# Channel mixing of the first batch element in plain block products, and Strassen weight sums made after it: an attention and mixer kernel on one Trainium2 core

## The chip, the cores and the metric

The kernel runs on one core of a Trainium2 chip. The metric is the device time of one execution in microseconds (us); less is better. One execution was also recorded by the hardware profiler, and all views of the profile come from it. The engines are named as there: PE is TensorE (PEld its weight loads), DVE is VectorE, ACT is ScalarE, POOL is GpSimd, and SP is the engine whose queue issues most of the transfers (DMAs).

## What is computed

Eight batch elements, each with 12 heads, 448 positions and a head size of 64, go through attention with normalized queries and keys. Its output, put together as 448 x 768 per element, goes through a mixer: first over the positions, then over the channels. The reference, cut:

```
def rmsnorm(x, g):
    rms = np.sqrt(np.mean(x * x, axis=-1, keepdims=True) + 1e-06)
    return x / rms * g
scores = scale * np.matmul(rmsnorm(q, g_q), rmsnorm(k, g_k).transpose(0, 1, 3, 2))
attn = np.exp(scores - np.max(scores, axis=-1, keepdims=True))
attn = attn / (np.sum(attn, axis=-1, keepdims=True) + 1e-09)
x = np.matmul(attn, v)                        # then (B, S, H*D)
h = np.maximum(x.transpose(0, 2, 1) @ w_tok1, 0.0) @ w_tok2
u = x + h.transpose(0, 2, 1)
out = u + np.maximum(u @ w_ch1, 0.0) @ w_ch2
```

All is float32, but the four weights come as float64; the kernel turns them into float32 itself, out of the bits of two 32-bit words. `w_ch1` is 768 x 1536, `w_ch2` 1536 x 768.

## The kernel before

**Start** (`Start.__init__`, L828) clears tiles, loads the queries and keys of the first two pairs of heads, and makes the norms of pair 0: `squares` (L900) squares on ACT and sums on DVE, `rsqrt` (L942) takes ten small DVE instructions. For pair 0 the queries' half is done first, then the keys'. A comparison of g_q and g_k picks one of two arms of the program (L986); with this data it is the one where `shifted` is False.

**Attention** goes by pairs of heads, six pairs to a batch element, 48 in all; two pairs take four steps (`att_step`, L461). A step has scores on PE, exponentials on ACT (`exp`, L291), and products with the values on PE (`av`, L397) for scores of the step before. Ahead of a pair's first step its queries are scaled (`scale`, L262, on POOL), and queries and keys are transposed on PE and copied by ACT (`trans_qk`, L274; in `before` that is an item of its own after the step, L532 to L534). Keys are not scaled; their norm goes into the exponential. From the second element on, the row sums are gathered by POOL and DVE (`chunk_sums`, L359).

**Mixing** of an element: transposes (`trans_x`, L553), `tok1` (L560), `tok2` (L571), which adds onto the element's tile `uT` in DVE (L579), then `ch1` (L635) and `ch2` (L689). The last two are Strassen products in Winograd's form: the weights and the moving matrix are cut into quarters, and seven products of half-size matrices, with sums of quarters before and after, take the place of eight. The moving sums are made by DVE and POOL (`moving_sums`, L587; in `ch1` L652 to L686), those after the products by L652 and L713. `ch2` comes as a double group (two of three column blocks) and a single one. A `ch1` item has two blocks of three matmuls of 224 columns, with 128 x 128 weights.

**Weights.** The two channel matrices come in 36 chunks, four that hold the token weights come before (`weight_chunks`, L118). A chunk is loaded by SP (`weight_load`, L145) into one of five `raw` tiles, goes through three instructions on DVE (`convert_first`, L189 to L192), two on ACT (`convert_second`, L200, L202), one on DVE (`convert_bits`, L209) and one on POOL (`convert_last`, L224), which leaves four quarters in a `stage` tile. `combine` (L160) then has POOL make the weights' sums of quarters, L163, L164 and L166, so that the tile has the seven stationary matrices; `store` (L168) writes them to a DRAM scratch (`ws1`, `ws2`, `ws3`). From there SP loads them again as `unit` tiles of 384 KB, five of them, for every one of the eight elements (`unit`, L608), in the order of `PRODUCTS` (L585). A unit is not loaded ahead before its group of chunks is stored.

**Order.** Each engine works through its instructions in the order in which they are written; there is no reordering. The order comes from `merge` (L29), which interleaves lists of items so that each list advances in proportion to the costs that stand beside its items. First come element 0's attention and 14 items of weights (L802); then, for each element, its mixing merged with the next element's attention (L805 to L820). In element 0 the rest of the weights is merged into the mixing too, so that the chunks of `w_ch1` and `w_ch2` are ready in time for their first use. SP's queue is written in the same way: a transfer that has to wait holds all behind it.

Of the kernel before, what the change touches and what calls it, by code (L numbers as in the profile page):

```python
# [22 lines left out]


NQ = 7
# [21 lines left out]
def whole(ctx, tc, shifted, pre, q, k, v, g_q, g_k, moe_w_tok1, moe_w_tok2, moe_w_ch1, moe_w_ch2, out):  # L47
# [28 lines left out]
    UNITS = 5  # L76
# [67 lines left out]

    def weight_load(i):  # L145
        rows, srcs, dst, split = chunks[i]
        n = columns(i) // len(srcs)
        wide = srcs[0].dtype == I64
        t = raw_pool.tile([P, WCOLS, 2] if wide else [P, WCOLS], U32 if wide else F32, name="raw")
        for k, src in enumerate(srcs):  # L150
            to = t[0:rows, k * n:(k + 1) * n]
            if wide:
                src = src.bitcast(U32)
                to = to.rearrange("p (i n) w -> p i (n w)", i=2) if dst is None else to.rearrange("p n w -> p (n w)")
            elif dst is None:
                to = to.rearrange("p (i n) -> p i n", i=2)
            nc.sync.dma_start(out=to, in_=src)
        st["raw", i] = t

    def combine(j):  # L160

        q = st["stage", j]
        nc.gpsimd.tensor_tensor(out=q[:, 6], in0=q[:, 1], in1=q[:, 0], op=ALU.subtract)  # L163
        nc.gpsimd.tensor_tensor(  # L164
            out=q[:, 4:6], in0=q[:, 1:7:5], in1=q[:, 3:4].to_broadcast([P, 2, P]), op=ALU.add)
        nc.gpsimd.tensor_tensor(out=q[:, 1], in0=q[:, 2], in1=q[:, 5], op=ALU.subtract)  # L166

    def store(j):  # L168


        w, group, m, t = stages[j]
        q = st.pop(("stage", j))
        if group < 3:
            to = ws1[group, :, :, t, m % 2, :]
        elif group == 3:
            to = ws3[:, :, t, :]
        else:
            to = ws2[t // 3, :, :, t % 3, m, :]
        nc.sync.dma_start(out=to.rearrange("q p n -> p q n"), in_=q[:])
        st["stored"] = j if j + 1 < len(stages) else j + 1  # L180

# [30 lines left out]
    def convert_last(i):  # L212
        rows, srcs, dst, split = chunks[i]
        n = columns(i)
        if dst is None:
            q = st["stage", i - len(first)] = stage_pool.tile([P, NQ, P], F32, name="stage")
            dst = q[:, 0:4, :].rearrange("p q n -> p (q n)")
        fold = (lambda a: a.rearrange("p (r c) -> p r c", c=split)) if split else (lambda a: a)
        t = st.pop(("raw", i))
        if srcs[0].dtype != I64:  # L220
            nc.gpsimd.tensor_copy(out=dst, in_=fold(t[0:rows, 0:n]))
        else:
            lo, hi = (fold(t[0:rows, 0:n, w].bitcast(F32)) for w in range(2))
            nc.gpsimd.tensor_tensor(out=dst, in0=lo, in1=hi, op=ALU.mult)  # L224
        if i >= len(first):
            combine(i - len(first))

# [34 lines left out]
    def scale(p):  # L262

        n = 2 * NS
        qk, rs = st["qk", p], st["rs", p]
        parts = [(R, 0, n, rs[0:R, 0:n].unsqueeze(2))]
        if shifted:
            parts.append((P, n, n - 2, rs[:, n:2 * n - 2].unsqueeze(2)))
            parts.append((P, 2 * n - 2, 2, rs[:, 2 * n - 2:2 * n - 1].unsqueeze(2)))
        for rows, o, m, r in parts:  # L270
            x = qk[0:rows, o * D:(o + m) * D].rearrange("p (r d) -> p r d", d=D)
            nc.gpsimd.tensor_tensor(out=x, in0=x, in1=r.to_broadcast([rows, m, D]), op=ALU.mult)  # L272

    def trans_qk(p, i):  # L274
        qk = st["qk", p]
        if i == 0:
            st["qkT", p] = qkT_pool.tile([P, S + NS * P], F32, name="qkT")
        ps = s_tile("t_ps")
        n = P if i else R
        for c in range(NS):  # L280
            o = (i * NS + c) * P
            nc.tensor.transpose(ps[:, c * n:(c + 1) * n], qk[0:n, o:o + P], ident[0:n, 0:n])  # L282
        to = st["qkT", p][:, S:S + NS * P] if i else st["qkT", p][:, 0:S]
        nc.scalar.mul(to, ps[:, 0:NS * n], g_t[:, i:i + 1])  # L284
        if i == 1:
            st.pop(("qk", p))
# [43 lines left out]
    def score_shifted(p):  # L330
# [4 lines left out]
        for c in range(NS):  # L335
            for a in range(2):
# [11 lines left out]
                pt = m_tile()  # L348
# [112 lines left out]
    def att_step(g):  # L461
# [48 lines left out]
        def tiled():  # L510
            if shifted:
                if live:
                    both_shifted()
                return
            if live:
                scores()
            products()

        items.append((3.75 if s in (0, 3) else 2.25, tiled))
# [12 lines left out]
        q = p + (s + 1) // 2  # L532
        if live and s % 2 == 1 and q < NP:
            items += [(0.4, lambda i=i: trans_qk(q, i)) for i in range(2)]  # L534
# [50 lines left out]
    PRODUCTS = ((0, "B11"), (2, "B21"), (5, "T2"), (6, "T3"), (4, "T1"), (1, "B22"), (3, "T4"))  # L585
# [14 lines left out]
    def unit_list(b):  # L600

        flat = lambda a: a.rearrange("p a b n -> p (a b n)")
        l = [(mp, flat(ws1[mp, q])) for mp in range(KF // 2) for q, _ in PRODUCTS]
# [4 lines left out]
    def unit(u):  # L608

        while st["loaded"] < min(u + UNITS, len(units)):  # L610
            i = st["loaded"]
            group, src = units[i]
            if st.get("stored", 0) < stage_end[group] and i > u:
                break
# [3 lines left out]
        return st.pop(("unit", u))  # L618

    def next_unit():  # L620
        st["at"] += 1
        return unit(st["at"] - 1)
# [8 lines left out]
    def put_off_done():  # L631
        while late_work:
            late_work.pop(0)()

# [118 lines left out]
    def middle_items(b):  # L753

        items = []
        for t in range(KC):
            items += [(us(NJ, S), lambda cc=cc: tok2(b, cc)) for cc in (t, KC + t)]
            items.append((0.0, lambda t=t: moving_sums(b, t)))
# [3 lines left out]
    def last_items(b):  # L762


        single = [(us(6, HS), lambda i=i: ch2(b, 1, i, 0)) for i in range(7)]
        l = turns(b, [0, 1, KC, KC + 1])
# [9 lines left out]
    st["loaded"] = st["at"] = 0  # L776
    r, late_work = {}, []
# [5 lines left out]

    load_v(0)
    weight_load(0)
    weight_load(1)
    scale(0)

    nc.vector.tensor_scalar(g_t[:, 0:1], g_t[:, 0:1], float(D) ** 0.5, None, ALU.mult)
    trans_qk(0, 0)  # L790
    trans_qk(0, 1)
# [4 lines left out]
    pre.squares(1, st)  # L796
    pre.roots(1, 1, st)
    swap(1)
    scale(1)
    per = NPAIR * 2  # L800
    att_items = lambda lo, hi: [it for g in range(lo, hi) for it in att_step(g)]
    for _, fn in merge(att_items(0, AHEAD * per + 1), weight_items(0, BEFORE)):  # L802
        fn()
    left = []
    for b in range(B):  # L805
        early, double = middle_items(b)
        if b == 0:
            begin = [it for h in range(2) for it in x_items(0, h) + tok1_items(0, h)]
            early = merge(begin + early, weight_items(BEFORE, then)) + merge(
                double, weight_items(then, len(chunks) + 3))  # L810
        else:

            for _, fn in merge(tok1_items(b, 0), left):
                fn()
            early = tok1_items(b, 1) + early + double
# [9 lines left out]
class Start:  # L825


    def __init__(self, ctx, tc, q, k, g_q, g_k, w2):  # L828
# [20 lines left out]
        for qk in [self.st["qk", p] for p in range(2)] + self.qk_t:  # L849
            nc.vector.memset(qk[96:P, 0:n // 2], 0.0)  # L850
            o = n - 2 * D
            nc.vector.memset(qk[D:P, o:o + D], 0.0)
            nc.vector.memset(qk[0:D, o + D:o + 2 * D], 0.0)
        self.load_qk(0, self.st, other=nc.scalar)
        self.load_qk(1, self.st)
# [15 lines left out]
        with tc.tile_pool(name="st_0", bufs=1) as self.st_pool:  # L871
            self.nt_pool = self.st_pool
            self.squares(0, self.st, halves=((0, 1), (1, 2)))
            self.st.pop(("ms", 0))

# [4 lines left out]
    def load_qk(self, p, st, other=None):  # L880
# [15 lines left out]
        for a in range(2):  # L896
            o = 4 * NS * D - 2 * D + a * D
            (other or self.nc.sync).dma_start(out=qk[a * D:(a + 1) * D, o:o + D], in_=self.k[b, hs][a][nk:])

    def squares(self, p, st, halves=((0, 2),)):  # L900
# [9 lines left out]
        for lo, hi in halves:  # L910
# [12 lines left out]
            if len(halves) > 1:  # L923
# [97 lines left out]
```

## Time and profile before

| | |
|---|---|
| median of 3 runs | 1482.06 us (1481.83 to 1483.47) |
| the profiled execution | 1482.08 us |
| its span, first to last instruction | 1480.3 us |
| PE busy, matmuls | 1394.3 us, 94% |
| DVE busy | 718.4 us, 49% |
| ACT busy | 470.7 us, 32% |
| POOL busy | 475.4 us, 32% |
| mean granted clock of PE | 0.975 |
| DMA | 214.77 MB, 145 GB/s mean |

How to read it: a busy share is a mean over the whole span, and the stages here differ. The views that follow give the span in 40 equal slices, each digit the busy share in tenths; a table by stretches of time, with the busy time of each engine, the number of its instructions, the clock that PE was granted (1 is full speed), the share of time that the 16 DMA engines were busy and what they moved; the waits of an engine, in total, how often, and the longest; and the chain of work that ended last, each line with its start, its length and what it was. A float32 matmul is two records on PE, so two MATMUL rows are one product. PE's busy time counts from issue to a modelled end and is longer where the clock is low.

### The profile page before, as it was taken

What the parts mean: (1) busy time and instruction counts of PE and PEld (TensorE: products, weight loads), DVE (VectorE), ACT (ScalarE), POOL (GpSimd) and SP (SyncE); (2) the same over time, 40 slices, a digit from 0 to 9 for tenths busy, and PEclk for the clock granted to TensorE, in tenths of its full rate; (3) what the DMA queues carried; (4) which work ended last, traced back from release to release, by engine and by line L of the source; (5) the groups of instructions that cost most, each with busy time, mean ns of one, the idle gap of its engine ahead of it and who ended that gap; (6) DMA issues with size and microseconds to landing.
All of it is one profiled execution on the core that took longest, in us unless ns stands there. A gap on an engine that the chain in (4) does not pass through costs nothing.

```text
span 1480.3 us, 19461 instructions
## 1 busy us (share of the span) xinstructions
PE 1394.3 (94%) x7048; PEld 1040.6 (70%) x7048; DVE 718.4 (49%) x1303; ACT 470.7 (32%) x802; POOL 475.4 (32%) x460
## 2 busy tenths in 40 slices
PE   5868767799999999999999999999999999999998
PEld 2324446586777867786777857777677947778998
DVE  7888897833454255433544345432544334331321
ACT  5654343322332234323342233322333223312111
POOL 2455686731233124321333123320332212310321
PEclk9988888899999999999999999999999999999999
DMA  6676677762455524553354625454354624444454
GB/s 151 168 213 183 192 238 216 212 196 84 122 149 144 159 76 138 147 151 112 106 155 127 181 56 153 132 152 130 103 148 124 179 62 128 122 124 134 128 172 135
DMA packets 235212, 214.77 MB, mean 145 GB/s; under 512 B 107140, under 2 KB 191620, under 8 KB 235108
## 3 DMA queue, kind: packets, MB, share of 16 engines
q1 hardware_dynamic: 211746, 202.20, 47.5%
q10 hardware_dynamic: 23234, 11.24, 2.7%
q8 instruction: 58, 0.95, 0.3%
q14 instruction: 46, 0.38, 0.1%
q0 software_dynamic: 128, 0.00, 0.0%
HBM read 185.86 MB, written 27.53 MB: 144 GB/s over the span
## 4 chain that ended last, share of the span: by engine, by line
PE 80%; POOL 1%; DMA 1%; DVE 1%; issue 1%; ACT 0%; SPq 0%; ACTq 0%; POOLq 0%
PE m_ps L704 26%; PE m_ps L647 23%; PE s_ps L302 7%; PE o_ps L403 6%; PE m_ps L566 5%; PE m_ps L574 4%; PE t_ps L545 3%; PE d_ps L382 2%; PE t_ps L282 2%; PE s_ps L316 1%; PE o_ps L415 1%; DMA unit<-ws 0%; POOL stage L224 0%; DMA ws<-stage 0%; POOL stage L164 0%
## 5 line engine op out<-in xcount | busy, mean ns | idle before, releaser
L704 PE MATMUL m_ps<-hb,unit 128*128 128x224 f32 x2016 | 402.7, 355 | 8.8 <-DMA unit<-ws 8.8
L704 PEld LDWEIGHTS m_ps<-hb,unit 128*128 128x128 f32 x2016 | 376.0, 191 | 28.7 <-issue 17.1
L292 ACT ACTIVATE e<-s_ps,rs 128x448 f32<-128x448 f32 x336 | 187.4, 633 | 214.2 <-PE s_ps L302 142.3
L647 PE MATMUL m_ps<-tu,unit 128*128 128x224 f32 x1152 | 238.9, 360 | 0.0
L647 PEld LDWEIGHTS m_ps<-tu,unit 128*128 128x128 f32 x1152 | 218.5, 194 | 15.7 <-PE o_ps L403 4.9
L647 PE MATMUL m_ps<-uT,unit 128*128 128x224 f32 x864 | 178.3, 359 | 9.3 <-DVE hb L652 6.1
L647 PEld LDWEIGHTS m_ps<-uT,unit 128*128 128x128 f32 x864 | 162.7, 192 | 28.8 <-issue 17.1
L302 PE MATMUL s_ps<-qkT 64*128 64x448 f32 x576 | 139.6, 588 | 5.9 <-ACT qkT L284 5.2
L272 POOL TENSOR_TENSOR qk<-qk,rs 112x512 f32<-112x512 f32 x46 | 51.1, 1132 | 265.5 <-DVE rs L951 189.2
L713 POOL TENSOR_TENSOR uT<-uT,r 128x448 f32<-128x448 f32 (+1 forms) x64 | 57.0, 901 | 245.6 <-DVE r L713 160.1
L403 PE MATMUL o_ps<-e,v 128*64 128x448 f32 x576 | 132.1, 562 | 0.0
L363 POOL TENSOR_TENSOR es<-e 128x896 f32<-128x896 f32 x42 | 88.3, 2102 | 63.3 <-ACT sq L913 47.6
L713 DVE TENSOR_TENSOR uT<-uT,m_ps 128x448 f32<-128x448 f32 (+1 forms) x80 | 38.9, 502 | 130.0 <-PE m_ps L704 127.8
L652 DVE TENSOR_TENSOR r<-m_ps,r 128x448 f32<-128x448 f32 x72 | 44.8, 622 | 117.6 <-POOL r L652 67.1
L566 PE MATMUL m_ps<-x,w_sb 112*128 112x384 f32 x256 | 92.4, 508 | 9.5 <-DVE x L551 9.5
L444 DVE STREAM_TRANSPOSE dt<-d_ps 128x448 f32<-128x448 f32 x42 | 27.3, 650 | 152.3 <-PE d_ps L382 152.3
L284 ACT ACTIVATE qkT<-t_ps,g_t 128x448 f32<-128x448 f32 x96 | 60.6, 657 | 127.3 <-PE t_ps L282 127.2
L369 DVE TENSOR_TENSOR es<-es,e 128x896 f32<-128x896 f32 x42 | 48.0, 1143 | 106.6 <-ACT e L292 75.8
L302 PEld LDWEIGHTS s_ps<-qkT 64*128 64x128 f32 x576 | 49.7, 191 | 68.3 <-issue 54.6
L403 PEld LDWEIGHTS o_ps<-e,v 128*64 128x64 f32 x576 | 33.0, 137 | 87.8 <-issue 85.0
L653 ACT ACTIVATE hb<-hb 128x448 f32<-128x448 f32 x72 | 41.7, 579 | 156.2 <-DVE hb L652 132.6
L574 PE MATMUL m_ps<-w_sb,h 128*128 128x448 f32 x192 | 80.0, 562 | 6.6 <-DVE uT L579 6.6
(85 smaller groups left out, 1478.2 us busy)
## 6 DMA issues: line engine op xcount, KB each, us to landing
unit<-ws SPq DMA_DIRECT2D x336, 384.0 KB, 3.2
raw<-in_moe_w_ch_dram SPq DMA_DIRECT2D x72, 256.0 KB, 3.3
ws<-stage SPq DMA_DIRECT2D x36, 448.0 KB, 3.3
out_dram<-y ACTq DMA_DIRECT2D x48, 224.0 KB, 3.3
qk<-in_q_dram SPq DMA_DIRECT2D x92, 112.0 KB, 3.2
v<-in_v_dram SPq DMA_DIRECT2D x48, 192.0 KB, 2.8
qk<-in_k_dram SPq DMA_DIRECT2D x92, 96.0 KB, 3.2
raw<-in_moe_w_tok_dram SPq DMA_DIRECT2D x4, 448.0 KB, 5.1
```

The costliest lines, as they stand in the source:

```text
L272: nc.gpsimd.tensor_tensor(out=x, in0=x, in1=r.to_broadcast([rows, m, D]), op=ALU.mult)
L284: nc.scalar.mul(to, ps[:, 0:NS * n], g_t[:, i:i + 1])
L292: nc.scalar.activation(out=out, in_=ps[:, 0:S], func=AF.Exp, scale=st["rs", p][:, r:r + 1])
L302: nc.tensor.matmul(out=pss[a][:, 0:S], lhsT=qkT[a * D:(a + 1) * D, o:o + P], rhs=qkT[a * D:(a + 1) * D, 0:S], start=True, stop=True)
L363: nc.gpsimd.tensor_tensor(out=es[:], in0=st["e", p, 0][:], in1=st["e", p, 1][:], op=ALU.add)
L369: nc.vector.tensor_tensor(out=es[:], in0=es[:], in1=st["e", p, 2][:], op=ALU.add)
L403: nc.tensor.matmul(out=o[a * D:(a + 1) * D, 0:S], lhsT=vt[:, c:c + D], rhs=e[:, a, :], start=start, stop=stop)
L566: nc.tensor.matmul(out=ps[:, 0:HC], lhsT=w1_sb[0:R, c, jc * P:(jc + 1) * P], rhs=st["x", h][0:R, c, :], start=(c == 0), stop=(c == NS - 1))
L574: nc.tensor.matmul(out=ps[:, 0:S], lhsT=st["h1", jc][:, cc * P:(cc + 1) * P], rhs=w2_sb[:, jc].rearrange("p c r -> p (c r)"), start=(jc == ...
L647: nc.tensor.matmul(out=ps[:, j * HS:(j + 1) * HS], lhsT=w[:, t, j, :], rhs=m, start=(t == 0), stop=(t == KC - 1))
L704: nc.tensor.matmul(out=ps[:, j * HS:(j + 1) * HS], lhsT=st["w"](j, t), rhs=hb[:, HB[what], t, :], start=(t == 0), stop=(t == KF - 1))
L713: add = lambda e, o, x, y: e.tensor_tensor(out=o, in0=x, in1=y, op=ALU.add)
```

## The change

Four things are done.

1. **Element 0's channel mixing** takes the eight plain products: `ch1_first` and `ch2_first` multiply the stored quarters with all 448 columns of `uT` and add up in PSUM. No moving sums and no sums after are made for element 0, but one addition per column block of the result. Element 0 uses 24 units in place of 42.
2. **The weights' sums** leave the conversion: `combine` is gone, a chunk is stored as four quarters. `sum_items` makes the sums afterwards, 40 items for 36 stages: an item reads a stage's four quarters back from DRAM into one of the five `raw` tiles, makes a subtraction on DVE, two additions in one on POOL and a subtraction on DVE for the three stages before, and writes the four sums of the stage before those. Eight items are merged into the double part of element 0, the rest into `tok2` and `ch1` of element 1. The scratch has eight slots a stage. There are six `unit` tiles, and `load_units` is called in the sum items too.
3. **The start**: the tiles' clearing is cut down and partly moved to POOL, an ACT instruction at the very start brings the table load forward, the keys of pair 0 are transposed first, the queries' norms come ahead of the keys', the queries of pair 0 are scaled on DVE. The norms and scaling of pair 1 come after the first attention step.
4. **The transposes of the next pair** stand between scores and products of a step, in place of after it, in the attention of element 0 (`inside`).

The diff, cut to its core:

```
-NQ = 7
+NQ = 8
-    UNITS = 5
+    UNITS = 6
...
-    def combine(j):
-
-        q = st["stage", j]
-        nc.gpsimd.tensor_tensor(out=q[:, 6], in0=q[:, 1], in1=q[:, 0], op=ALU.subtract)
-        nc.gpsimd.tensor_tensor(
-            out=q[:, 4:6], in0=q[:, 1:7:5], in1=q[:, 3:4].to_broadcast([P, 2, P]), op=ALU.add)
-        nc.gpsimd.tensor_tensor(out=q[:, 1], in0=q[:, 2], in1=q[:, 5], op=ALU.subtract)
...
+    def sum_items():
+        def one(i):
+            n = len(stages)
+            if i < n:
+                t = raw_tile()
+                q = st["sum", i] = t[:].rearrange("p n w -> p (n w)").bitcast(F32).rearrange(
+                    "p (q n) -> p q n", q=NQ)
+                st["sum tile", i] = t
+                nc.sync.dma_start(out=q[:, 0:4], in_=slots(i, 0, 4))
+            if 0 <= i - 1 < n:
+                q = st["sum", i - 1]
+                nc.vector.tensor_tensor(out=q[:, 6], in0=q[:, 1], in1=q[:, 0], op=ALU.subtract)
+            if 0 <= i - 2 < n:
+                q = st["sum", i - 2]
+                nc.gpsimd.tensor_tensor(
+                    out=q[:, 4:6], in0=q[:, 1:7:5], in1=q[:, 3:4].to_broadcast([P, 2, P]), op=ALU.add)
+            if 0 <= i - 3 < n:
+                q = st["sum", i - 3]
+                nc.vector.tensor_tensor(out=q[:, 7], in0=q[:, 2], in1=q[:, 5], op=ALU.subtract)
+            if 0 <= i - 4 < n:
+                nc.sync.dma_start(out=slots(i - 4, 4, 8), in_=st.pop(("sum", i - 4))[:, 4:8])
+                st.pop(("sum tile", i - 4))
+                st["summed"] = i - 4 if i - 4 < n - 1 else n
+                load_units(st["at"])
+        return [(1.0, lambda i=i: one(i)) for i in range(len(stages) + 4)]
...
             if live:
                 scores()
+            if inside:
+                for i in range(2):
+                    trans_qk(q, i)
             products()
...
+        inside = turned and g < 2 * NPAIR - 1 and not shifted
...
+    def load_units(u):
+        while st["loaded"] < min(u + (UNITS - 2 if u < first_units else UNITS - 1), len(units)):
             i = st["loaded"]
             group, src = units[i]
-            if st.get("stored", 0) < stage_end[group] and i > u:
+            ready = st.get("stored" if i < first_units else "summed", 0)
+            if ready < stage_end[group] and i > u:
                 break
...
+    def ch1_first(mp, o, j):
+        u = st["uT", 0]
+        if j == 0:
+            st["w"] = next_units(2)
+        ps = m_tile()
+        for t in range(2 * KC):
+            nc.tensor.matmul(
+                out=ps[:, 0:S], lhsT=st["w"][t // KC][:, t % KC, j, :], rhs=u[:, t, :],
+                start=(t == 0), stop=(t == 2 * KC - 1))
+        nc.scalar.activation(
+            out=natural(o)[:, :, 2 * mp + j, :], in_=ps[:, 0:S].rearrange("p (i n) -> p i n", i=2),
+            func=AF.Relu)
...
+    def ch2_first(o, half, m):
...
+        if half:
+            u = st["uT", 0][:, o * KC + m, :]
+            nc.vector.tensor_tensor(out=u, in0=u, in1=st.pop(("m", m))[:, 0:S], op=ALU.add)
...
+        trans_qk(0, 1)
+        scale(0, nc.vector)
+        pre.squares(0, st, halves=((1, 2),))
+        trans_qk(0, 0)
...
+            att_items(0, 1) + [(0.0, second_pair)] + att_items(1, AHEAD * per + 1), weight_items(0, BEFORE)):
...
             early = merge(begin + early, weight_items(BEFORE, then)) + merge(
-                double, weight_items(then, len(chunks) + 3))
+                double, weight_items(then, len(chunks) + 3) + sums[:8])
...
+            if b == 1:
+                early = merge(early, sums[8:])
...
+        warm = const.tile([P, 1], F32, name="warm")
+        nc.vector.memset(warm[:], 1.0)
+        nc.scalar.activation(out=warm[:], in_=warm[:], func=AF.Square)
+        self.zeros(nc.vector, self.st["qk", 0])
         self.load_qk(0, self.st, other=nc.scalar)
+        for i, qk in enumerate([self.st["qk", 1]] + self.qk_t):
+            eng = nc.gpsimd if i else nc.vector
+            self.zeros(eng, qk)
+            eng.memset(qk[96:P, 0:n // 2], 0.0)
```

## The prediction

> **What bounds the kernel now.** I read the slices first, then the table by stretches, then what TensorE waited for, then the chain that ended last.
>
> ```profile
> PE   5868767799999999999999999999999999999998
> DVE  7888897833454255433544345432544334331321
> POOL 2455686731233124321333123320332212310321
> PEclk9988888899999999999999999999999999999999
> ```
>
> Each slice is 37 us. From the tenth on TensorE (PE) is full at full clock and nothing else matters; in the first nine it has holes, its granted clock is low, and VectorE (DVE) is the fullest engine beside it. Any gain must come from there, and anything put later costs only if it stops a full PE.
>
> ```profile
> core 0: us, PE busy (x) PEld busy (x) DVE busy (x) ACT busy (x) POOL busy (x), PEclk, DMA share, GB/s
> 16.50:105.00 88.50, 75.26 (x368) 28.63 (x368) 74.25 (x139) 56.33 (x93) 36.70 (x41) 0.92 0.63 173
> 105.00:274.00 169.00, 121.23 (x500) 80.59 (x500) 144.22 (x197) 66.08 (x112) 118.90 (x125) 0.84 0.69 209
> 274.00:342.00 68.00, 67.19 (x360) 57.49 (x361) 32.99 (x57) 18.77 (x32) 26.95 (x30) 0.96 0.67 202
> 342.00:1480.30 1138.30, 1128.77 (x5813) 872.38 (x5812) 457.08 (x870) 325.76 (x560) 288.61 (x251) 1.00 0.46 130
> ```
>
> I call these stretches A (attention of element 0), B (its token mixing and `ch1`, attention of element 1 beside), C (its `ch2`) and the rest. In B, DVE is busy 144 of 169 us (85%) while PE's busy time at full clock is 121.2 x 0.84 = 102 us. B is paced by DVE, and 67 us longer than PE needs. A is 74 of 88.5 DVE against 69 PE. C is already PE: 67 of 68.
>
> ```profile
> PE d_ps L382 <- ACT e L292: 17.0, 3, 6.5
> PE m_ps L566 <- DVE x L551: 9.5, 2, 5.5
> PE m_ps L704 <- DMA unit<-ws: 8.8, 2, 8.3
> PE m_ps L647 <- DVE hb L652: 6.1, 2, 4.7
> PE s_ps L316 <- ACT qkT L284: 5.8, 2, 4.2
> ```
>
> These waits (to 330 us) lead back to work on DVE, or on ACT queued behind a weight conversion that waits for DVE (`ACT e_t L200 <- DVE e_t L192`, 65.5 us). From 330 us on PE waited 3.6 us in all.
>
> ```profile
> 315.71 3.61 DMA ws<-stage
> 319.32 0.02 issue
> 319.34 2.93 DMA unit<-ws
> 322.27 0.14 issue
> 322.41 2.51 PE m_ps L704 x12
> ```
>
> The chain before C's end: a transfer on SP's queue that depends on another does not start until that has landed, 3.61 us after its issue. This decides the price of the new work below.
>
> **What the skill says.** *SBUF — State Buffer* (the port pair that DVE and GpSimd share) calls it an exclusive lock held for a whole instruction: the loser blocks. The trace agrees: L190 (two SBUF inputs) takes 0.69 us at its shortest and 1.34 at its median, whenever POOL's L224 runs; L192 0.39 and 0.56. *DMA: Bandwidth & Descriptors* (Two DMAs through the same engine are not ordered) says that only the completion semaphore orders two transfers, also on one queue; the chain above agrees. *TensorE: Matmul & The Clock Gate* (HAM oscillation) says that idle gaps lower PE's clock; here 0.84 in B and 1.00 at the end, so fewer gaps pay twice. Prices: *VectorE: DVE Perf Modes* (the errata section) gives (N+151)/0.96 ns for an fp32 tensor_tensor: 624 ns at N=448, which L450 takes.
>
> **The change, part by part.** The profiled execution took 1482.08 us (span 1480.3 and 1.8 around), the median of the runs is 1482.06; the sum is made against 1482.1.
>
> *Plain products for element 0: PE.* 12 records (6 matmuls of 224 columns) take 2.27 us, so 0.378 us each. Seven products are 252 matmuls = 95.3 us; eight are 144 matmuls of 448 columns = 144 x 0.757 = 109.0. PE gets +13.7 us, half in B, half in C.
>
> *DVE in B.* Gone are element 0's sums: L652 15 instructions 9.3 us, L677 5.3, L595 and L596 4.3: 18.9. `ch2_first` adds 6 x 0.62 = 3.7, in C, where 14 of L713 (7) go.
>
> *POOL in B.* `combine` goes: L163, L164, L166, 25 each, 18.8 + 20.2 + 16.4 = 55 us; and 20 of element 0's sums. POOL falls from 119 to some 45. This alone ends nothing, POOL was not full; what counts is DVE's waiting at the lock. L224 stays, and it is L224 that meets L190, so L190 keeps its 1.34. What should go: L192 25 x 0.13 = 3, L209 from 0.88 towards its median 0.68, 24 x 0.15 = 4, L189 4, others (L921, L369, L374) 3: 14 us, between 5 and 30 (all of the excess except L190's).
>
> B: DVE 144 - 19 - 14 = 111; PE 102 + 7 = 109. At the 85% that the bound reaches today, B lasts 111 / 0.853 = 130 us: **-39**. Two engines full together wait more for each other (0.80: 139, -30), fewer gaps give a better clock (0.92: 121, -48). I take -38.
>
> *A.* The same 14 chunks are converted. About half have their `combine` here (7 x 2.1 us of POOL), so DVE saves some 3. The transposes of the next pair move between scores and products, so that ACT's qkT runs under the products; the two waits on ACT qkT are 11.0 us in the page of waits, most of it here. Its other side: `trans_qk` now stands ahead of `av`; if `scale` on POOL is late, the products wait too. **-7**, from 0 to -14.
>
> *The start.* First score at 16.49 us. The table load (1.28) and the keys' rsqrt (about 1.5 between the queries') leave the path, and DVE scales in some 0.7 for POOL's 1.08: 3 to 4 us earlier. But pair 1's squares, roots and `scale` are now queued after step 0, behind its exponentials and pair 2's squares: 1.1 ACT + 1.2 DVE twice, 2.2 roots, 1.1 POOL lie before a `trans_qk` that the products of step 1 stand behind; before, they ran while PE had step 0. I estimate that this eats most of it: **-1** (+2 to -4). The memsets on POOL go ahead of its loads of g_t and of the identity by some 2.5 us, early enough (before: 1.25 to 4.2; transposes at 9 or later).
>
> *C.* PE +6.9; of the 8.3 us wait for `ws3`'s last store some 3 go, since the last weights are spread over fewer items. Eight sum items lie here, one per 4 us beside the weights. **+4** (-4 to +7).
>
> Together up to 342 us: -42, between -20 and -60.
>
> *The sums, 28 of 36 in element 1.* PE there was full, so this is the open item. Compute: DVE 2 x 0.29 us by the page's price (to 0.62, the 128x224 row L596), POOL 0.82 (L164): DVE is at 50% and POOL at 30% there, hidden. The queue: each item issues, on SP, a read R(i), then a write W(i-4). The tile of R(i) is the fifth of five: it is free only when W(i-5), issued one item earlier, has landed. So SP turns in one issue (0.37) plus one landing per item. No row shows a write of 256 KB in 512-byte rows; the nearest are `out_dram<-y` (224 KB, 3.3 us) and `ws<-stage` (448 KB, 3.3; shortest 2.7). R's bytes go ahead of W's. Period: 3.1 at the least, 4.8 when DMA is crowded as at 100 to 120 us (277 GB/s, landings to 7.4); I take **3.9**.
>
> How much time has an item? They are spread evenly over `tok2` and `ch1` of element 1: 56 us of PE, and attention in proportion: (56 + 32) / 124.5 of its costs, 0.71 of 46 us = 33; 89 to 91 us in all, by 32 items: 2.83 us each. Queued behind a waiting SP are the units; and DVE's first subtraction of an item waits for R, issued one item before, with PE's sums (L652) behind it. With two `m_ps` buffers PE cannot run away from DVE, so PE goes at SP's pace: 28 x (3.9 - 2.83) = **+30**. Least 28 x 0.27 = +8, most 28 x 1.97 = +55. DMA says the same from another side: 28 reads and 32 writes of 256 KB, 21 units of 384 KB and some 2.7 MB for attention are 27 MB; in 91 us that is 295 GB/s, above what a crowded stretch reached, in 121 us 220.
>
> Sum: 1482.1 - 42 + 30 = **1470**.
>
> **Rivals.**
> 1. *The sums hide.* Landings near 2.7 us, or SP ahead by more than an item, leave +8 or less; with -42, 1448. For it: the shortest ws landing. Against it: SP waits for PE at every qk and v load (L892 <- PE t_ps L282, 46.8 us from 340 to 700), so it is never far ahead.
> 2. *Slower: the sum loop at SP.* The same loop at 4.8 us per item: +55, so 1495. It turns the sign at 42 / 28 + 2.83 = 4.3 us per item. For it: landings of transfers on ws of 3.5 us median with tails to 7.4 from 60 to 150 us, and units and qk loads in the same engines. Against it: landings of 3.1 median (units, after 340 us).
> 3. *Early stays as it was paced.* If DVE, blocked by L224, or the weights' own pipeline sets B, only half of the 42 comes: 1482 - 20 + 30 = 1492. Against it: DVE's removed instructions are certain.
>
> **How the numbers follow.** The main case 0.45 (1455 to 1484 alone; a fifth of it within 3 us of before or above); rival 1 0.27; rival 2 0.18; rival 3 0.10. 0.2%, about what a measurement can tell from no change, is 3 us. Faster: 0.36 + 0.27 = 0.63; same: 0.06 from the main case, 0.02 from the rivals' edges = 0.08; slower 0.29. The range, 1436 to 1498, takes in rival 1 with a better clock, and rival 2; it leaves out a DMA that collapses, and early gains near 60 with hidden sums.
>
> **What would show it.** Element 1's `tok1` (L566, at 342.9 us before) begins near 301; PEclk in B rises above 0.9; B near 130 us with no POOL rows for sums of weights. In element 1's `tok2` and `ch1`, 89 us of PE stretch to some 120, waits of DVE on the reads and of PE on DVE appear, and sum items come every 3.9 us on SP. I am wrong if that stretch stays under 100 us, or if B stays above 145.

## The result, and the profile after

| | before | after |
|---|---|---|
| device time, median of 4 runs | 1482.09 us (1481.83 to 1483.47) | 1484.35 us (1483.25 to 1485.92) |
| span of the profiled execution | 1480.3 us | 1481.7 us |
| mean granted clock of TensorE | 0.975 | 0.984 |

The ratio is 1.0014, with a 95% interval of 0.9997 to 1.0032: no difference that can be measured, where 1470 was forecast. The slices of the kernel after, as in the prediction's first view:

```profile
PE   4887889999889999999999999999999999999998
DVE  5787868616565255533544345432544334331321
POOL 2222323304453123321333123320332212310320
PEclk9898999999999999999999999999999999999999
```

POOL is at about half or less of what it was in slices 4 to 8, DVE has fallen in the sixth (9 to 6) and the eighth (8 to 6), PE is at 9 from the seventh slice on instead of the ninth, and its clock is higher. So the work that was to leave POOL and DVE is gone. But PE now has a new hole, 8 and 8 in slices 11 and 12. The stretches (the first number is the length in us, then each engine's busy time, PE's clock, the DMA share, GB/s):

```profile
core 0: us, PE busy (x) PEld busy (x) DVE busy (x) ACT busy (x) POOL busy (x), PEclk, DMA share, GB/s
12.20:115.60 103.40, 77.32 (x368) 30.78 (x368) 78.09 (x151) 58.15 (x97) 24.74 (x20) 0.91 0.60 160
115.60:248.40 132.80, 117.75 (x388) 53.11 (x388) 104.92 (x158) 58.49 (x101) 40.85 (x31) 0.93 0.64 184
248.40:321.70 73.30, 73.10 (x262) 36.70 (x261) 39.02 (x66) 21.06 (x35) 17.60 (x15) 1.00 0.65 187
335.80:447.30 111.50, 96.26 (x459) 66.08 (x458) 71.86 (x152) 33.64 (x57) 52.75 (x54) 0.97 0.80 233
```

The first three are A, B and C, cut at TensorE's first scores, at element 0's first `tok1` product (L596, before L566), at its first `ch2` product and at element 1's first `tok1` product; the last is `tok2` and `ch1` of element 1. The prediction's B began at 105 us; here it begins with `tok1`, 5.5 us later in the kernel before. Against the kernel before, cut at the same instructions (changes are taken before rounding):

| mark or stretch | before | after | change | predicted |
|---|---|---|---|---|
| first scores begin | 16.5 | 12.2 | -4.3 | -3 to -4 |
| element 0's `tok1` begins | 110.5 | 115.6 | +5.2 | -8 (start and A) |
| B | 163.8 | 132.8 | -31.0 | -38 |
| C | 68.5 | 73.3 | +4.8 | +4 |
| element 1's `tok1` begins | 342.8 | 321.7 | **-21.0** | -42 |
| element 1, to element 2's `tok1` | 168.6 | 190.4 | **+21.8** | +30 |
| of it, `tok2` and `ch1` | 86.1 | 111.5 | +25.4 | +30 |
| the rest | 969.0 | 969.6 | +0.6 | 0 |

The gain is there at 321.7 us and gone at 512.1. `tok2` and `ch1` of element 1 lose more than the element does, since they now hold some attention that stood beside its `ch2`, which is 3 us shorter.

**In B**, where DVE's groups for the conversion of weights show what it was relieved of. The columns are line, operation, count, then busy us and mean ns of one, then idle time before them. Kernel before:

```profile
L190 DVE SCALAR_TENSOR_TENSOR raw<-raw,e_t 128x512 f32<-128x512 uint32 x24 | 31.9, 1330 | 1.7
L209 DVE SCALAR_TENSOR_TENSOR raw<-raw,e_t 128x512 uint32<-128x512 uint32 x24 | 21.0, 876 | 0.9 <-ACT e_t L200 0.8
L189 DVE TENSOR_SCALAR e_t<-raw 128x512 uint32<-128x512 uint32 x24 | 18.3, 762 | 0.8
L192 DVE TENSOR_SCALAR e_t<-raw 128x512 uint32<-128x512 uint32 x24 | 14.6, 610 | 0.8
```

Kernel after:

```profile
L216 DVE SCALAR_TENSOR_TENSOR raw<-raw,e_t 128x512 f32<-128x512 uint32 x23 | 29.7, 1292 | 2.1 <-DVE e_t L215 0.5
L218 DVE TENSOR_SCALAR e_t<-raw 128x512 uint32<-128x512 uint32 x23 | 16.9, 734 | 0.8
L235 DVE SCALAR_TENSOR_TENSOR raw<-raw,e_t 128x512 uint32<-128x512 uint32 x23 | 16.5, 717 | 3.5 <-ACT e_t L226 3.4
L215 DVE TENSOR_SCALAR e_t<-raw 128x512 uint32<-128x512 uint32 x23 | 13.3, 577 | 0.8
```

Two rows fall by 160 and 185 ns, the first stays (it still meets POOL's multiplication), and the mean of L218 rises by 124 ns where the prediction had it falling by 130. The mean hides two groups. Of its 23 instructions 19 take 0.43 us, which is the forecast 0.13 less than the 0.56 that was usual before; the other four take 2.19 us each, and each of the four lies beside an addition of exponentials on POOL (L386), which now starts at another point of DVE's order. One of them, the first line on DVE and the second on POOL:

```profile
178.59 2.19 DVE L218 TENSOR_SCALAR e_t<-raw 128x512 uint32<-128x512 uint32 x1
177.97 2.52 POOL L386 TENSOR_TENSOR es<-e 128x896 f32<-128x896 f32 x1
```

All of DVE in B is 139.0 us before (to 274.2) and 104.9 after. The prediction took off 33 us, which from 139.0 leaves 106.

B of the kernel before has a second part that the prediction misplaced. Its last 8.3 us are a wait of PE for the first unit of `ch2`, and the chain there goes through POOL's multiplication and `combine`:

```profile
265.55 1.20 POOL stage L224
266.81 0.79 POOL stage L163
...
269.81 4.30 DMA unit<-ws
274.25 1.83 PE m_ps L704 x4
```

The prediction read this as a wait for `ws3` inside C and let some 3 us of it go; the wait for `ws3` was 0.6 us. In the kernel after PE does not wait at this place.

**Ahead of it**, PE's two largest waits in the kernel after, to 125 us (in all, times, longest):

```profile
PE t_ps L305 <- POOL hb L295: 10.1, 1, 10.1
PE t_ps L305 <- POOL stage L250: 9.2, 2, 6.3
```

The first is pair 1: its transposes wait for queries whose scaling is queued behind step 0, and step 1's products stand behind them. The second is not what its name says. The timeline there (start, duration, in brackets the idle time before and who ended it):

```profile
59.71 2.49 POOL L295 TENSOR_TENSOR qk<-qk,rs 112x512 f32<-112x512 f32 x2 [4.68 <-DVE rs L1063]
...
61.33 2.15 DVE L215 TENSOR_SCALAR e_t<-raw 128x512 uint32<-128x512 uint32 x1
62.16 1.03 POOL L250 TENSOR_TENSOR stage<-raw 128x512 f32<-128x512 f32 x1
...
64.83 0.72 ACT L226 ACTIVATE e_t<-e_t,expo_c 128x512 uint32<-128x512 uint32 x1 [5.43 <-DVE e_t L218]
...
66.02 2.18 ACT L315 ACTIVATE e<-s_ps,rs 128x448 f32<-128x448 f32 x4
...
66.74 1.83 PE L305 MATMUL t_ps<-ident,qk 112*128 112x112 f32 x8 [6.28 <-POOL stage L250]
```

The transposes start 0.1 us after the first exponential (L315) is done with its PSUM tile: scores and transposes share the tiles. The exponentials stand on ACT behind a conversion step that waited 5.43 us for DVE, and DVE's L215 itself took 2.15 us (the next one, at 65.37, takes 0.43) while POOL ran two scalings of queries (L295) and a multiplication of weights (L250).

**In element 1**, the waits from 340 to 450 us. SP's queue and DVE's first subtraction:

```profile
SPq L190 <- DMA ws<-raw: 24.6, 20, 2.8
SPq L202 <- DVE raw L200: 17.6, 16, 2.8
DVE raw L193 <- DMA raw<-ws: 36.1, 18, 4.5
```

Reads (L190) wait for the landing of a write, writes (L202) for the subtraction (L200), subtractions (L193) for the reads. Before the change PE waited for nothing in this stretch; now it is idle for 15.2 of 111.5 us, for the most part for work on DVE, which stands behind those subtractions. The two largest waits:

```profile
PE m_ps L726 <- DVE hb L731: 4.5, 2, 2.8
PE m_ps L726 <- DVE r L731: 3.7, 3, 3.0
```

The chain there shows the circle of a write, a read, two subtractions and the next write:

```profile
383.11 4.67 DMA ws<-raw
387.80 3.53 DMA raw<-ws
391.42 0.29 DVE raw L193
391.71 0.20 DVE raw L200
...
400.94 3.87 DMA ws<-raw
```

In the gap lie 5 us of DVE's work for attention, a sum of products and the subtractions of the next item, so the subtractions themselves are short but not free of what stands around them. SP's queue also does not take reads and writes strictly in turn, as `sum_items` writes them:

```profile
398.92 1.38 SPq L202 DMA_DIRECT2D ws<-raw  x1
400.94 0.39 SPq L202 DMA_DIRECT2D ws<-raw  x1
402.47 0.36 SPq L190 DMA_DIRECT2D raw<-ws  x1
404.88 0.36 SPq L190 DMA_DIRECT2D raw<-ws  x1
```

Two writes stand ahead of two reads, so that two landings run side by side. The order on the engine is thus not in every place the one in which the program is written.

### The profile page after: what moved, and what is told of

Same layout as the page of the kernel before. It is cut to its first block, busy times and chain, and to the rows that moved or that the text cites. A ratio compares the mean times of both kernels' runs of the same rounds, so it can differ in the third digit from the quotient of the medians.

```text
span 1481.7 us, 19089 instructions
## 1 busy us (share of the span) xinstructions
PE 1404.9 (95%) x6832; PEld 995.9 (67%) x6832; DVE 711.5 (48%) x1332; ACT 466.8 (32%) x798; POOL 402.1 (27%) x370
## 4 chain that ended last, share of the span: by engine, by line
PE 82%; DVE 8%; DMA 5%; issue 1%; SPq 1%; ACT 1%; POOL 1%; ACTq 0%; DVEq 0%; POOLq 0%
PE m_ps L783 23%; PE m_ps L726 21%; PE s_ps L325 7%; PE o_ps L426 7%; PE m_ps L596 5%; PE m_ps L707 4%; PE m_ps L604 4%; PE t_ps L575 3%; PE m_ps L689 3%; PE t_ps L305 2%; DMA ws<-raw 2%; DMA raw<-ws 2%; PE d_ps L405 2%; PE s_ps L339 1%; PE o_ps L438 1%
## 5 line engine op out<-in xcount | busy, mean ns | idle before, releaser
L783 PE MATMUL m_ps<-hb,unit 128*128 128x224 f32 x1764 | 349.5, 354 | 0.0
L783 PEld LDWEIGHTS m_ps<-hb,unit 128*128 128x128 f32 x1764 | 327.8, 190 | 16.2 <-issue 12.7
L315 ACT ACTIVATE e<-s_ps,rs 128x448 f32<-128x448 f32 x336 | 186.8, 632 | 208.6 <-PE s_ps L325 143.0
L726 PE MATMUL m_ps<-tu,unit 128*128 128x224 f32 x1008 | 204.8, 354 | 2.1 <-DVE hb L731 1.8
L726 PEld LDWEIGHTS m_ps<-tu,unit 128*128 128x128 f32 x1008 | 187.6, 190 | 12.2 <-PE o_ps L426 4.2
L726 PE MATMUL m_ps<-uT,unit 128*128 128x224 f32 x756 | 156.9, 361 | 7.2 <-DVE r L731 3.5
L726 PEld LDWEIGHTS m_ps<-uT,unit 128*128 128x128 f32 x756 | 142.7, 192 | 26.3 <-issue 16.4
L295 POOL TENSOR_TENSOR qk<-qk,rs 112x512 f32<-112x512 f32 x46 | 51.5, 1141 | 293.8 <-DVE rs L1063 181.0
L792 POOL TENSOR_TENSOR uT<-uT,r 128x448 f32<-128x448 f32 (+1 forms) x56 | 51.1, 922 | 229.3 <-DVE r L792 147.9
L386 POOL TENSOR_TENSOR es<-e 128x896 f32<-128x896 f32 x42 | 89.7, 2136 | 67.2 <-ACT sq L1025 52.7
L596 PE MATMUL m_ps<-x,w_sb 112*128 112x384 f32 x256 | 92.5, 507 | 8.9 <-DVE x L581 8.9
L307 ACT ACTIVATE qkT<-t_ps,g_t 128x448 f32<-128x448 f32 (+1 forms) x96 | 60.8, 658 | 122.4 <-PE t_ps L305 120.6
L1029 DVE TENSOR_REDUCE ms<-sq 128x16 f32<-128x1040 f32 (+2 forms) x49 | 59.2, 1207 | 52.5 <-ACT sq L1025 49.4
L731 DVE TENSOR_TENSOR r<-m_ps,r 128x448 f32<-128x448 f32 x63 | 39.2, 621 | 94.2 <-POOL r L731 54.5
```

Of the source, the lines that this page charges most:

```text
L315: nc.scalar.activation(out=out, in_=ps[:, 0:S], func=AF.Exp, scale=st["rs", p][:, r:r + 1])
L386: nc.gpsimd.tensor_tensor(out=es[:], in0=st["e", p, 0][:], in1=st["e", p, 1][:], op=ALU.add)
L596: nc.tensor.matmul(out=ps[:, 0:HC], lhsT=w1_sb[0:R, c, jc * P:(jc + 1) * P], rhs=st["x", h][0:R, c, :], start=(c == 0), stop=(c == NS - 1))
L726: nc.tensor.matmul(out=ps[:, j * HS:(j + 1) * HS], lhsT=w[:, t, j, :], rhs=m, start=(t == 0), stop=(t == KC - 1))
L783: nc.tensor.matmul(out=ps[:, j * HS:(j + 1) * HS], lhsT=st["w"](j, t), rhs=hb[:, HB[what], t, :], start=(t == 0), stop=(t == KF - 1))
L792: add = lambda e, o, x, y: e.tensor_tensor(out=o, in0=x, in1=y, op=ALU.add)
```

## Experiments

The kernel before, measured again beside runs 1 to 4, 5 to 8 and 9 to 11, had medians of 1483.22, 1482.76 and 1482.72 us; each ratio is to it, with its 95% interval. Marks and views come from the one profiled execution of a run: in runs 4, 5 and 9, which leave A as the change made it, `tok1` of element 0 begins at 113.7 to 114.3 us, against 115.6 in the kernel after, so that a mark can be off by 2 us. My theory: the early gain is real, the sums take it back in element 1, and start and A lose by pair 1's place and by the new place of the transposes. The rival: the sums are covered, and only half of the early gain came, for reasons of B.

**1. Pair 1 before step 0.**

```
+    second_pair()
     per = NPAIR * 2
...
-            att_items(0, 1) + [(0.0, second_pair)] + att_items(1, AHEAD * per + 1), weight_items(0, BEFORE)):
+            att_items(0, AHEAD * per + 1), weight_items(0, BEFORE)):
```

> The changed kernel, with the norms and the scaling of pair 1 put back ahead of the first attention step. Theory (the start lost its 4 us because these stand in the queues behind step 0 and the products of step 1 behind the transposes that need them): the 10.1 us wait of PE at 27.3 us goes, element 1's tok1 begins 5 to 9 us earlier than 321.7, time 1475 to 1479. Rival (attention of element 0 is paced by the 14 chunks on DVE, a hole more or less at the start is taken back): under 2 us, 1482 to 1485.

Measured: 1477.21 us, 0.9958 (0.9944 to 0.9972). Element 0's `tok1` begins at 108.6, 7.1 earlier than after, element 1's at 313.9, 7.8 earlier. Held: with the transposes where the change has them, the place of pair 1 costs 7 us.

**2 and 3. Transposes behind the products again; and both together.**

```
-        inside = turned and g < 2 * NPAIR - 1 and not shifted
+        inside = False
```

> The changed kernel, with the transposes of the next pair back behind the products of the step. Theory (in the new place they need PSUM tiles that the step's own exponentials still hold, and ACT's exponentials stand behind a weight conversion, so that the products wait too): the waits at 66.7 and 96.2 us (9.2 us together) shrink to the 3 us that the kernel before had, time 1478 to 1482. Rival (the new place hides ACT's copy, 11 us of waits before): the waits on qkT come back and the time is 1485 to 1492.

> Both of these undone, the rest of the change kept. If both theories hold: the sum of the two gains, 9 to 14 us, 1470 to 1475, and element 0's tok1 begins near 104 instead of 115.6. If attention of element 0 is paced by DVE's conversions: within 3 us of the changed kernel.

Measured: 1482.46, 0.9998 (0.9989 to 1.0007), `tok1` at 111.3; both together 1481.76, 0.999 (0.998 to 0.9999), `tok1` at 112.7. PE's waits in run 2 to 125 us, its start left out:

```profile
PE s_ps L325 <- ACT qkT L307: 5.1, 4, 2.0
PE s_ps L339 <- ACT qkT L307: 3.9, 1, 3.9
PE t_ps L305 <- POOL stage L250: 2.6, 1, 2.6
```

The wait for tiles shrinks from 9.2 to 2.6 us, and waits for `qkT` come back, 9.0 us in place of 1.8. The profiled execution of run 3 is one of its slower ones (1484.55), so its mark is late. By the medians:

| | pair 1 late | pair 1 early |
|---|---|---|
| transposes inside the step | 1484.35 (after) | 1477.21 (run 1) |
| transposes after the step | 1482.46 (run 2) | 1481.76 (run 3) |

The two edits don't add; they depend on each other. With pair 1 early the new place of the transposes is worth 4.5 us. With pair 1 late it is worth nothing (1.9 us the other way, which the intervals do not separate). And pair 1's late place costs 7 us only with the transposes inside the step, where the products stand behind them; otherwise 0.7, not separated either. So my theory that the transposes' place was a harm is not borne out, and the rival's 1485 to 1492 did not come either. Run 3 is within 3 us of the kernel after, as expected if conversions pace this stretch.

**4. No sums.** Elements 1 to 7 multiply plain quarters (not the computation):

```
-    PRODUCTS = ((0, "B11"), (2, "B21"), (5, "T2"), (6, "T3"), (4, "T1"), (7, "B22"), (3, "T4"))
+    PRODUCTS = ((0, "B11"), (2, "B21"), (1, "T2"), (2, "T3"), (0, "T1"), (3, "B22"), (3, "T4"))
...
-                double, weight_items(then, len(chunks) + 3) + sums[:8])
+                double, weight_items(then, len(chunks) + 3))
...
-            if b == 1:
-                early = merge(early, sums[8:])
```

> The changed kernel without the sums of weights: they are left out, elements 1 to 7 multiply with plain quarters where they should use sums. Theory (the loop of reads and writes on SP stretches element 1 by 22 us): from element 1's tok1 to element 2's takes 168 to 170 us instead of 190.4, and the eight items in element 0 cost some 1 us, time 1460 to 1463. Rival (part of the 22 us comes from DMA and buffers of element 1 as such, or element 0's late weights): under 15 us of gain, 1470 or more.

Measured: 1457.73, 0.9828 (0.9812 to 0.9845). Element 1 takes 168.6 us, as before the change; B and C 202.5, against 206.1 after. The sums cost 26.6 us in all by the medians: 21.8 in element 1, 3.6 in B and C by the marks. The theory held, the rival fell. Within those 202.5 us B is 120.8 and C 81.7, where after has 132.8 and 73.3: two waits of PE in B, 6.1 and 3.9 us, are gone, and PE waits 6.5 us for a unit in C instead.

**5. The sums' results in tiles of their own**, so that a read doesn't wait for the write of the item before:

```
-                nc.vector.tensor_tensor(out=q[:, 6], in0=q[:, 1], in1=q[:, 0], op=ALU.subtract)
+                s = st["out", i - 2] = stage_pool.tile([P, 4, P], F32, name="stage")
+                nc.vector.tensor_tensor(out=s[:, 2], in0=q[:, 1], in1=q[:, 0], op=ALU.subtract)
...
-                nc.sync.dma_start(out=slots(i - 4, 4, 8), in_=st.pop(("sum", i - 4))[:, 4:8])
+                nc.sync.dma_start(out=slots(i - 3, 4, 8), in_=s[:])
```

> The changed kernel, with the four sums of a stage written into a stage tile instead of the tile of the quarters, so that a read no longer waits for the landing of the write before it, and with the first subtraction two items after the read instead of one. The bytes moved are the same. Theory (the 22 us in element 1 come from SP's loop of read and write): tok2 and ch1 of element 1 fall from 111.6 us to 92 to 98, time 1466 to 1472. Rival (they come from the 16 DMA engines, 86% busy there): still above 105 us, time above 1478.

Measured: 1478.81, 0.9971 (0.996 to 0.9983). `tok2` and `ch1` of element 1, and the waits in it:

```profile
334.30:434.10 99.80, 92.49 (x459) 64.89 (x458) 69.56 (x141) 31.27 (x54) 53.38 (x76) 0.98 0.84 247
```

```profile
DVE stage L194 <- DMA ws<-stage: 22.9, 10, 6.7
PE m_ps L781 <- DVE r L729: 5.1, 1, 5.1
```

11.7 us of the stretch go, but PE then waits 5.1 ahead of `ch2`, and at element 2's `tok1` only 3.5 are left (element 1 takes 186.9 us). Neither expectation came true. This leaves open how much is the circle and how much the bytes: the three stage tiles made a new wait for a landing, on DVE, in the old one's place.

**6. Plain products alone: `combine` back in the conversion, no sums afterwards.** Eight slots are stored at once, and there are two `stage` tiles instead of three:

```
+        if i >= len(first):
+            combine(i - len(first))
...
-        nc.sync.dma_start(out=slots(j, 0, 4), in_=st.pop(("stage", j))[:])
+        nc.sync.dma_start(out=slots(j, 0, NQ), in_=st.pop(("stage", j))[:])
```

> Plain products for element 0, but the weights' sums made by POOL in the conversion again and stored with the quarters (eight slots); no sum items. Theory (in B one half of the gain is DVE's removed sums of products, the other the lock with POOL's combine): B lasts 145 to 150 us instead of 132.8, element 1 takes 168.5, time 1473 to 1479. Rival (POOL's combine costs nothing, DVE's 19 us were all): B at 133 to 137 us, time 1461 to 1466.

Measured: **1468.14**, 0.9901 (0.9885 to 0.9918), which is between the two expectations. B and C take 209.4 us (B 124.0, which neither expectation had), and element 1 168.6. The largest wait of PE comes at 252 us, in element 0's `ch2`:

```profile
PE m_ps L718 <- DMA unit<-ws: 10.4, 1, 10.4
```

B and C were 232.3 before. So with plain products they are 22.9 us shorter, without `combine` 6.9 more (209.4 to 202.5 of run 4), and eight of the sums give 3.6 back: 206.1. By the medians runs 6 and 4 differ by 10.4 us. This difference is `combine` together with twice the bytes of each store and one `stage` tile less; which of them makes the wait above longer than run 4's 6.5 us was not tested.

**7 and 8. What sets A.** Run 1 with pair 2's loads ahead of the weights' and values' on the queues, and run 1 with six chunks of weights moved from A into B:

```
+    pre.load_qk(2, st)
     load_v(0)
...
-    BEFORE = len(first) + 10
+    BEFORE = len(first) + 4
```

> As the run with pair 1 prepared early, and pair 2's queries and keys loaded ahead of the values and the first weights on SP. Theory (the 4.3 us by which the first scores come earlier are lost because ACT's squares of pair 2 wait for that load, with the exponentials of step 1 behind them): the first denominator comes 2 to 4 us earlier than 35.5 us, time 1473 to 1476. Rival (values or weights are then late instead): 1476 to 1480.

> As the run with pair 1 prepared early, with six of the 14 conversions taken out of element 0's attention and put into its mixing. If attention of element 0 is paced by the conversions (ACT's exponentials behind them), tok1 begins 14 to 22 us earlier than 108.6, and the mixing takes as much longer, time within 5 us of 1477. If it is paced by attention's own chain, tok1 comes at most 6 us earlier and the time grows by 8 us or more.

Measured: 1480.33, 0.9983 (0.9976 to 0.9989), and 1473.98, 0.9942 (0.9925 to 0.9958). Earlier loads made A longer (`tok1` at 111.8 against 108.6), so that theory fell; what they made late was not found. Fewer chunks made it shorter, by as much as was expected if the conversions set its pace. The stretch A of run 8:

```profile
12.20:90.20 78.00, 69.47 (x369) 27.26 (x369) 59.64 (x127) 51.09 (x85) 17.30 (x14) 0.98 0.55 143
```

In run 1, A was 96.4 us with 78.13 of DVE's work. It is 18.4 us shorter with 18.5 less of that work: DVE's idle time is 18.3 in both. So A shrank by what DVE no longer did, though DVE is busy for 76% of it only. The six chunks also take 7.0 us of work from ACT, 7.4 from POOL, and their loads, so the run shows that the conversions set the pace of A, not that DVE's part of them alone does. Most comes back in B and C: element 1's `tok1` begins 5.9 us earlier than in run 1, the median is 3.2 lower.

**9. Half the bytes.** The sums read and write two slots of four, with the same instructions (wrong sums, and two products read other slots):

```
-                nc.sync.dma_start(out=q[:, 0:4], in_=slots(i, 0, 4))
+                nc.sync.dma_start(out=q[:, 0:2], in_=slots(i, 0, 2))
...
-                nc.sync.dma_start(out=slots(i - 4, 4, 8), in_=st.pop(("sum", i - 4))[:, 4:8])
+                nc.sync.dma_start(out=slots(i - 4, 4, 6), in_=st.pop(("sum", i - 4))[:, 4:6])
```

> The changed kernel, with reads and writes of the sum items cut to two of four slots (128 KB each, rows of 512 bytes as before); the sums are then made of the wrong quarters, and two products use other slots. Waits, order and number of transfers are the same. If the 22 us in element 1 come from the latency of the loop, tok2 and ch1 of element 1 take 104 to 110 us (111.6 in the changed kernel); if from the bytes, 90 to 97 us. If from both, between.

Measured: 1464.68, 0.988 (0.9864 to 0.9897). Element 1 takes 173.0 us, 4.4 more than without sums; `tok2` and `ch1` take 93.7, within what was expected if the bytes decide. Two of the waits from 335 to 430 us:

```profile
SPq L190 <- DMA ws<-raw: 8.8, 9, 3.0
DVE raw L193 <- DMA raw<-ws: 8.6, 6, 2.8
```

The circle has as many links as before, and these waits fall from 24.6 and 36.1 us to 8.8 and 8.6. So most of the loss goes with the bytes, and the count of instructions and transfers alone doesn't make it. How the bytes act is less clear: the median landing fell only from 3.7 to 3.2 us for the writes and from 3.6 to 3.5 for the reads, while the DMA engines' load fell too, from 80% to 67% of the stretch.

**10 and 11. Put together:** run 6 with pair 1 early and six chunks later; and the same with ten (`BEFORE = len(first)`).

> Plain products for element 0 with POOL's combine in the conversion (1468.1), pair 1 prepared early (-7 in its own run) and six chunks later (-3). If the three act on different stretches: 1456 to 1461. If the attention of element 0 and the mixing trade the same DVE time: 1464 to 1469.

> As the one put together, with all ten chunks of the channel weights out of element 0's attention. Attention of element 0 then has little to wait for and should be 8 to 14 us shorter still; if PE has room in the mixing the time is 1452 to 1458, if the first products then wait for their weights it is 1460 to 1468.

Measured: **1460.95**, 0.9856 (0.9839 to 0.9872), faster than both kernels and as expected if the three act apart; and 1487.1, 1.0028 (1.002 to 1.0035), slower than either expectation. In the second, `tok1` begins no earlier (89.0 against 86.6), and the weights come late:

```profile
PE m_ps L700 <- DMA unit<-ws: 20.7, 2, 18.9
PE m_ps L718 <- DMA unit<-ws: 14.2, 1, 14.2
```

## Why the prediction was wrong

It summed to -12; the profiled spans differ by +1.4: +5.2 (start and A), -31.0 (B), +4.8 (C), +21.8 (element 1), +0.6 (rest).

- **"The start: -1" and "A: -7" are the steps that failed**, 13 us together: -8 was forecast and +5.2 measured. First scores came 4.3 us earlier, as predicted. Two terms after that were wrong. Pair 1's place, named as the other side and put at about 3 us, cost 7 (run 1). And the gain of 7 from the transposes' new place was counted as if it were independent of pair 1: it exists, 4.5 us, only when pair 1 is ready early (runs 1 and 3). With pair 1 late the products wait behind the transposes, and nothing is gained (run 2). What the prediction did not price is that the conversions set the pace of A (run 8), and the change left them there, 78.1 us of DVE's work against 79.7. So even with pair 1 early (run 1) A takes 96.4 us, against 94.0 before. Where these 2 us go was not traced; single executions differ by as much.
- **B: -38, measured -31.0.** DVE's and PE's work came out as predicted (104.9 for 106; 117.75 x 0.93 = 110 us at full clock for 109). The term that was off is the share at which DVE was to bind: kept at 85%, at which B would have lasted 123 us, and measured at 79%. This share is no fixed property of B: with the same work in B it is 86% without the sums (run 4, B 120.8) and 90% with `combine` back (112.1 of 124.0, run 6). In the kernel after, the eight sum items stand in the list of C, yet B has two more waits of PE, 6.1 and 3.9 us; they are part of the order that `merge` makes, but how was not traced. And 8.3 us of B's gain are the wait for the first `ch2` unit, which the prediction had booked in C.
- **C: +4, measured +4.8.** The number is in part luck: its wait for weights was not in C, and run 4 shows that time moves between B and C with the order of items. Together they were to give -34 and gave -26.2.
- **The sums: +30, measured +21.8.** That reads wait for landings held, and PE waits for DVE behind them. 111.5 us for 32 items is 3.48 us each, for 3.9 predicted (PE's own pace was taken as 2.83). The term to correct is the count of landings, not their size: the median landing of a write was 3.7 us, with one issue (0.36) 4.1 in each turn. SP stood waiting ahead of 20 reads, not of every one, and two writes were often under way side by side. At 3.48 us the prediction's own working gives (3.48 - 2.83) x 32 = 20.8 us, close to what was measured.
- **Rivals.** The sums did not hide (1). The loop did not reach 4.3 us per item, where the sign would have turned at a gain of 42 (2); but the gain was 21.0, and for that gain the turning point is 21.0 / 28 + 2.83 = 3.6 by the prediction's 28 items, and 3.5, what was measured, by the 32 of the stretch. Rival 3 names the amount that happened, half of 42, and got 0.10; its reason, the weights' own pipeline, fits A (run 8) and the wait at B's end before, but 13 of the 21 us that were missing lie in the start and A.
- **What I did not separate.** I priced plain products and `combine`'s removal as one gain in B. Runs 4 and 6 split it: 22.9 and 6.9 us in B and C. The removal that makes the sums necessary was worth 6.9 us by the marks, 10.4 by the medians, and the sums cost 26.6. Priced apart, the prediction would have said that one half of the change pays and the other doesn't.

In the Trainium skill, *SBUF — State Buffer* (SBUF: two separate sides) says that of a DVE and a GpSimd instruction that need the shared ports the second waits for the whole of the first; the four L218 of 2.19 us beside an L386 of 2.52, and two rows shorter by 160 and 185 ns without POOL's sums, agree. The formula in *VectorE: DVE Perf Modes* (The TRN2 errata) gives an estimate of 0.29 us for a subtraction of 128 elements; the trace has medians of 292 and 284 ns.

Open: how much of the sums' cost is the circle and how much DMA's load (runs 5 and 9 bound it from two sides), why sums in C's list lengthen B, what run 7 made late, and the last 2 us of A.

## What to carry to other kernels

Price what a change removes and what it puts in its place as a pair, apart from the edits that come with it: here 7 to 10 us were bought for 26.6. Work moved from beside an idle engine to beside a full one must fit there in every resource, and a loop that reads, changes and writes back through memory can be paced by its landings, however little it computes (here 3.5 us per item, for two subtractions of 0.3). Two edits to one queue are not priced one by one: the transposes' new place was worth 4.5 us or nothing, depending on what stood ahead of them. And a mean over one line's instructions can hide two groups.

## What was not expected of the hardware

- Transfers of 256 KB in 512-byte rows took 2.5 us (least), 3.6 to 3.7 (median) and 5.9 (most) to land in element 1, in a stretch with the DMA engines at 80% and 233 GB/s. With half the bytes of the sums, at 67% and 192 GB/s, the medians were 3.2 and 3.5 us, but the waits for them fell to about a third and a quarter.
- With one of two POOL streams gone, DVE's remaining instructions did not all get faster: four of 23 at L218 took 2.19 us in place of 0.43, each beside an addition on POOL that now started at another point of DVE's order.
- A wait for a free PSUM tile was recorded under the name of an instruction that has nothing to do with the tile (L305 <- POOL stage L250, 6.28 us); the timeline gave the true one, an exponential that ended 0.1 us earlier.
